# Moving the sums of x for u's seven products from VectorE to GpSimd, and writing variance plus epsilon as a scalar_tensor_tensor

## The chip, the cores and the metric

The kernel runs on one core of a Trainium2 chip. The metric is the device time of one execution in microseconds (us); lower is better. The engines are named as the profile names them: PE is the matrix engine (TensorE), PEld its loading of weights, DVE is VectorE, ACT is ScalarE, POOL is GpSimd, and SP issues DMAs.

## The reference

A linear attention without softmax, with a normalisation per head, feeds a gated layer with a spatial product. All tensors are float32.

```python
kv = np.einsum('bhsd,bhse->bhde', k, v)          # 8 batches, 8 heads, 576 rows, 64 columns
out = np.einsum('bhsd,bhde->bhse', q, kv)
rms = np.sqrt(np.mean(out * out, axis=-1, keepdims=True) + 1e-06)
x = out / rms * g_norm                            # then [8, 576, 512]
h = np.maximum(x @ w_in, 0.0)                     # 512 -> 1024
u, v = h[..., :512], h[..., 512:]
v_n = (v - mean(v)) / np.sqrt(var(v) + 1e-06)
v_s = np.einsum('ts,bsd->btd', w_spatial, v_n) + b_spatial[None, :, None]
out = (u * v_s) @ w_out
```

## The kernel before

**Precision.** Most products are made three times from a high and a low half of each operand (names ending in H and L). `split` makes the halves: ACT casts the high half (L327), DVE subtracts it for the low half (L328).

**Stages.** From batch b = 2 on, each batch runs through three stages on PE. `first(b)` makes v (`hv`, L324, PSUM tile `psh`) and u (`u_steps`, L546, tiles `psua`, `psub`, `psuc`). `second(b)` makes the spatial product (`sp_steps`, L546, L552 and L554, tiles `psa`, `psb`, `psc`) and `gate`s it with u into G (L565, L567, then a split). `last(b)` multiplies G by the output weights WO (`out_unit`, L291, shown as `pso<-WO,G`; each unit has four steps of K, three products each) and stores. The attention of later batches (L136, L211, and transposes L239 and L249 into `pstr` and `pstt`) is threaded between these steps.

**The sums of x.** u's products and the spatial products are made with seven block products instead of eight, by adding and subtracting blocks first. For u these are blocks of x: `x_sums_` runs once for each of the batches 2 to 7, with two rounds (k = 0, 1) of eight instructions on 128x288 blocks: four sums XH+XL (L440) into tiles p1, u2, u3 and g, then four differences (L442 to L445). Then `split` puts the results into T (L327 and L328, tile T, with a part of it in tile UX). T lies in the buffer of G, and UX in the buffer of WO, so the splits, and the DMA UX<-spare_u (L871, issued on POOL), wait until the out stage of the batch before has read G and WO for the last time. PE first reads T in `psub<-T` (L546), after `hv` and the first step of u.

**The normalisations.** `rsqrt_a` computes 1/sqrt(variance + epsilon): ACT takes the square root (L173), DVE adds epsilon (L174) and takes the reciprocal (L175), and `rsqrt_b` refines it (L180 to L182). It runs on 128x8 tiles for the heads and on 128x1 tiles for the layer norm.

**Order.** The first two batches follow a table (PLAN); the rest is written as loops. A scheduler that keeps a timeline of its own then sets the order of the instructions on each engine. `tc.issue_after(last_gate[0])` puts the sums behind a gate's last DVE instruction in that scheduler. Each engine runs its instructions strictly in the order given, so changed costs on one engine can change the order on all of them.

Of the kernel before, what the change touches and what calls it, by code (L numbers as in the profile page):

```python
# [8 lines left out]
F32 = mybir.dt.float32  # L9
# [4 lines left out]
ALU = mybir.AluOpType  # L14
# [5 lines left out]
P = 128  # L20
# [10 lines left out]
EPS = 1e-6  # L31
# [13 lines left out]
def f32(ap):  # L45
    return ap.bitcast(F32)
# [3 lines left out]
def body(ctx: ExitStack, tc, qT, kvm, kvt, g2, w_in, wsT, bsp, w_out, out):  # L50
    nc = tc.nc
# [48 lines left out]
    ident = persistent([P, P], F32, "ident")  # L100
    gcol = persistent([P, 16], F32, "gcol")[:, 0:1]
    edge = ctx.enter_context(tc.tile_pool(name="edge", bufs=1, side="right"))
    epsc = edge.tile([P, 8], F32, name="epsc", tag="epsc")[:, 0:1]

# [59 lines left out]
    def rsqrt(ss, n, rows, mul, tag):  # L166

        return rsqrt_b(*rsqrt_a(ss, n, rows, mul, tag))

    def rsqrt_a(ss, n, rows, mul, tag):  # L170
        a, s0, q, r = (small.tile([P, n], F32, name=f"{x}{tag}", tag=f"{x}{tag}")[0:rows]
                       for x in "asqr")
        nc.scalar.activation(s0, ss, AF.Sqrt, bias=epsc[0:rows], scale=mul)  # L173
        nc.vector.tensor_scalar(a, ss, mul, EPS, op0=ALU.mult, op1=ALU.add)  # L174
        nc.vector.reciprocal(q, a)  # L175
        return s0, q, r

# [10 lines left out]
    def norm_a(ps, rows=P, accumulate=False):  # L188
        x = work.tile([P, 512], F32, name="x", tag="x")[0:rows]
        ss = small.tile([P, 8], F32, name="ss", tag="ss")[0:rows]  # L190
        if accumulate:
            for h in range(8):
                cols = slice(h * D, (h + 1) * D)
                nc.scalar.activation(x[:, cols], ps[0:rows, cols], AF.Square,  # L194
                                     accum_out=ss[:, h:h + 1])
        else:
            nc.scalar.activation(x, ps[0:rows], AF.Square)
            nc.vector.tensor_reduce(ss, heads(x), axis=AX.X, op=ALU.add)
        return ps, x, rows, rsqrt_a(ss, 8, rows, 1.0 / D, "h")
# [126 lines left out]
    def split(hi, lo, x):  # L326
        nc.scalar.copy(hi, x)  # L327
        nc.vector.tensor_tensor(lo, x, f32(hi), op=ALU.subtract)  # L328
# [100 lines left out]
    def x_sums():  # L429

        with tc.issue_after(last_gate[0]):
            x_sums_()

    def x_sums_():
        for k in range(2):
            q = []
            for of, j, name in ((0, 0, "p1"), (2, 1, "u2"), (0, 1, "u3"), (2, 0, "g")):
                q.append(work.tile([P, HS], F32, name=name, tag=name))
                x = [f32(x[:, of + k, j * HS:(j + 1) * HS]) for x in (XH, XL)]
                nc.vector.tensor_tensor(q[-1], *x, op=ALU.add)  # L440
            q11, q22, q12, q21 = q
            nc.vector.tensor_tensor(q11, q12, q11, op=ALU.subtract)  # L442
            nc.vector.tensor_tensor(q12, q22, q12, op=ALU.subtract)
            nc.vector.tensor_tensor(q22, q22, q11, op=ALU.subtract)
            nc.vector.tensor_tensor(q21, q21, q22, op=ALU.subtract)  # L445
            for n, x in (1, q22), (0, q11), (2, q12), (3, q21):
                split(TH[n][:, k], TL[:, n, k], x)

# [340 lines left out]
        issue()  # L789

    nc.vector.memset(KVB[:, 1], 0.0)
    nc.vector.memset(epsc, EPS)
    nc.scalar.activation(small.tile([P, 1], F32, name="warm", tag="av"), epsc, AF.Sqrt)
    nc.gpsimd.memset(KVB[:, 0], 0.0)
    for kt in KT:
# [227 lines left out]
```

## Time and profile before

| | |
|---|---|
| median of 3 runs | 512.02 us (511.95 to 512.6) |
| the profiled execution's own time | 511.49 us |
| its span (first to last instruction) | 509.7 us |
| granted PE clock, mean | 0.998 |
| busy PE, DVE, ACT, POOL | 499.0, 411.5, 291.9, 21.4 us |

Sums and waits below come from this one profiled execution. Rows of the timeline give start, duration, engine, line and operation, with the idle time before it and what ended that in brackets. Rows of groups give the count, the busy time, the mean of one in ns, and the idle time before. Pipelined instructions overlap, so the distance between two starts is less than the duration of one.

### The profile page before, as it was taken

How to read it: one execution, taken by the hardware profiler on the slowest of the kernel's cores; microseconds unless marked ns; L12 is line 12 of the kernel's file. 1: busy time of each engine (PE TensorE's matmuls, PEld its weight loads, DVE VectorE, ACT ScalarE, POOL GpSimd, SP SyncE). 2: the span in 40 equal slices, each digit the busy share in tenths (PEclk: the TensorE clock that was granted, in tenths of full speed). 3: DMA queues.
4: the chain of work that ended last, by engine and by line, in shares of the span. 5: the costliest groups of instructions: out<-in, count | busy, mean ns of one | idle time of the engine just before them, and what ended most of it. 6: DMA issues, size and time to landing. Idle time of an engine off the chain costs nothing.

```text
span 509.7 us, 9917 instructions
## 1 busy us (share of the span) xinstructions
PE 499.0 (98%) x3436; PEld 439.0 (86%) x3436; DVE 411.5 (81%) x1265; ACT 291.9 (57%) x1021; POOL 21.4 (4%) x47
## 2 busy tenths in 40 slices
PE   7999999999999999999999999999999999999996
PEld 6658788898988899989998899988998889988995
DVE  3898599688998699968897779968898579987860
ACT  2555456896734696457732688447642578527422
POOL 5000000000000001000000001000000001000000
PEclk9999999999999999999999999999999999999999
DMA  8995300735346516345265514424354511314223
GB/s 254 330 339 191 100 24 1 236 91 176 116 152 209 186 42 212 118 117 174 76 218 196 187 42 154 152 91 164 123 178 146 167 39 44 145 42 165 70 98 104
DMA packets 28071, 72.24 MB, mean 142 GB/s; under 512 B 3506, under 2 KB 8626, under 8 KB 26484
## 3 DMA queue, kind: packets, MB, share of 16 engines
q1 hardware_dynamic: 24564, 49.58, 29.9%
q0 software_dynamic: 3456, 22.02, 12.6%
q8 instruction: 27, 0.44, 0.4%
q14 instruction: 24, 0.20, 0.1%
HBM read 58.48 MB, written 13.11 MB: 140 GB/s over the span
## 4 chain that ended last, share of the span: by engine, by line
PE 78%; ACT 8%; DVE 7%; DMA 4%; POOL 1%; issue 1%; SPq 0%; ACTq 0%; POOLq 0%; DVEq 0%
PE pso L291 15%; PE psh L324 12%; PE psb L546 6%; PE psub L546 5%; PE pso L211 5%; PE psc L546 4%; PE pskv L136 3%; PE psa L546 3%; PE psua L546 3%; PE psuc L546 3%; PE psu L402 3%; PE psa L411 3%; PE psh L378 3%; PE pstr L239 2%; ACT x L194 2%; DMA out<-o 1%
## 5 line engine op out<-in xcount | busy, mean ns | idle before, releaser
L291 PE MATMUL pso<-WO,G 128*128 128x512 f32 x384 | 97.3, 396 | 0.0
L291 PEld LDWEIGHTS pso<-WO,G 128*128 128x128 f32 x384 | 70.3, 188 | 14.1
L327 ACT CAST G<-g 128x288 fp32r<-128x288 f32 (+1 forms) x56 | 22.8, 408 | 61.2 <-DVE g L567 60.8
L194 ACT ACTIVATE x<-pso 128x64 f32<-128x64 f32 x208 | 44.3, 252 | 5.5 <-PE pso L211 5.3
L324 PE MATMUL psh<-WVL,XH 128*128 128x512 f32 x112 | 43.7, 390 | 0.0
L324 PE MATMUL psh<-WVH,XH 128*128 128x512 f32 x112 | 43.6, 393 | 0.0
L194 ACT ACTIVATION_READ_ACCUMULATOR x<-pso 128x1 f32 x208 | 43.5, 238 | 0.0
L324 PE MATMUL psh<-WVH,XL 128*128 128x512 f32 x112 | 43.4, 392 | 0.0
L328 DVE TENSOR_TENSOR VL<-v,VH 128x512 fp32r<-128x512 f32 (+1 forms) x56 | 34.2, 619 | 7.8 <-ACT VH L327 7.6
L648 ACT COPY o<-pso 128x512 f32<-128x512 f32 x35 | 20.3, 593 | 26.0 <-PE pso L291 23.5
L327 ACT CAST VH<-v 128x512 fp32r<-128x512 f32 (+1 forms) x56 | 31.1, 574 | 4.2 <-DVE v L356 3.8
L303 DVE BATCH_NORM_STATS2 s<-v 128x6 f32<-128x512 f32 x32 | 21.8, 690 | 7.3 <-ACT v L297 7.1
L546 PE MATMUL psb<-WSH,VH 128*128 128x288 f32 x84 | 25.4, 304 | 0.2
L311 ACT ACTIVATE v<-v,mv,rv 128x512 f32<-128x512 f32 x28 | 23.2, 837 | 3.2 <-DVE mv L310 3.2
L324 PEld LDWEIGHTS psh<-WVH,XH 128*128 128x128 f32 x112 | 21.0, 188 | 4.6 <-ACT o L648 0.2
L297 ACT ACTIVATE v<-psh 128x512 f32<-128x512 f32 x32 | 18.7, 595 | 10.9 <-PE psh L324 7.6
L324 PEld LDWEIGHTS psh<-WVL,XH 128*128 128x128 f32 x112 | 21.0, 188 | 4.6
L324 PEld LDWEIGHTS psh<-WVH,XL 128*128 128x128 f32 x112 | 21.0, 188 | 4.4
L546 PE MATMUL psb<-WSL,VH 128*128 128x288 f32 x84 | 24.6, 295 | 0.0
L546 PE MATMUL psb<-WSH,VL 128*128 128x288 f32 x84 | 24.3, 297 | 0.1
L328 DVE TENSOR_TENSOR G<-g,G 128x288 fp32r<-128x288 f32 (+1 forms) x56 | 23.4, 418 | 1.1 <-ACT G L327 0.4
L136 PEld LDWEIGHTS pskv<-KV 128*64 128x64 f32 x512 | 18.1, 140 | 6.7 <-issue 2.9
(243 smaller groups left out, 1426.2 us busy)
## 6 DMA issues: line engine op xcount, KB each, us to landing
KV<-kvm SPq DMA_DIRECT2D x31, 512.0 KB, 5.1
WO<-spare_o POOLq DMA_DIRECT2D x12, 1024.0 KB, 6.6
UX<-spare_u POOLq DMA_DIRECT2D x12, 768.0 KB, 6.0
out<-o SPq DMA_DIRECT2D x32, 256.0 KB, 2.2
qt<-qT SPq DMA_DIRECT2D x16, 288.0 KB, 4.3
stage<-w_in SPq DMA_DIRECT2D x8, 512.0 KB, 6.4
qt<-qT SPq DMA_DIRECT2D x16, 256.0 KB, 2.9
KT<-kvt SPq DMA_DIRECT2D x32, 64.0 KB, 4.7
```

What stands on the lines that cost most here:

```text
L136: return nc.tensor.matmul(ps[h:h + D, at:at + D], of[:, 0, h:h + D], of[:, 1, h:h + D], start=c == 0, stop=c == NC)
L194: nc.scalar.activation(x[:, cols], ps[0:rows, cols], AF.Square, accum_out=ss[:, h:h + 1])
L211: nc.tensor.matmul(ps[:, c * P:(c + 1) * P], qt[:, c * P:(c + 1) * P], st[p], start=True, stop=True)
L291: nc.tensor.matmul(ps, lt, rh, start=i == 0, stop=i == n - 1)
L297: nc.scalar.activation(v, ps, AF.Relu)
L303: nc.vector.bn_stats(s6, v)
L311: nc.scalar.activation(v, v, AF.Identity, bias=m, scale=r)
L324: nc.tensor.matmul(ps, lt, rh, start=k == 0 and i == 0, stop=k == NP - 1 and i == 2)
L327: nc.scalar.copy(hi, x)
L328: nc.vector.tensor_tensor(lo, x, f32(hi), op=ALU.subtract)
L546: nc.tensor.matmul(ps, lt, rh, start=start and i == 0, stop=stop and i == len(pairs) - 1, skip_group_check=True)
L648: nc.scalar.copy(o, ps)
```

## The change

The eight sums and differences of each round of `x_sums_` are issued on GpSimd instead of VectorE. In `rsqrt_a`, the tensor_scalar that multiplies by `mul` and adds the constant epsilon becomes a scalar_tensor_tensor that multiplies by `mul` and adds a tile `epsn` of 8 columns, which a memset fills with epsilon. All lines below the first edit move down by one: L440 of before is L441 after it.

```diff
-    epsc = edge.tile([P, 8], F32, name="epsc", tag="epsc")[:, 0:1]
+    epsn = edge.tile([P, 8], F32, name="epsc", tag="epsc")
+    epsc = epsn[:, 0:1]
...
-        nc.vector.tensor_scalar(a, ss, mul, EPS, op0=ALU.mult, op1=ALU.add)
+        nc.vector.scalar_tensor_tensor(a, ss, mul, epsn[0:rows, 0:n], op0=ALU.mult, op1=ALU.add)
...
-                nc.vector.tensor_tensor(q[-1], *x, op=ALU.add)
+                nc.gpsimd.tensor_tensor(q[-1], *x, op=ALU.add)
             q11, q22, q12, q21 = q
-            nc.vector.tensor_tensor(q11, q12, q11, op=ALU.subtract)
-            nc.vector.tensor_tensor(q12, q22, q12, op=ALU.subtract)
-            nc.vector.tensor_tensor(q22, q22, q11, op=ALU.subtract)
-            nc.vector.tensor_tensor(q21, q21, q22, op=ALU.subtract)
+            nc.gpsimd.tensor_tensor(q11, q12, q11, op=ALU.subtract)
+            nc.gpsimd.tensor_tensor(q12, q22, q12, op=ALU.subtract)
+            nc.gpsimd.tensor_tensor(q22, q22, q11, op=ALU.subtract)
+            nc.gpsimd.tensor_tensor(q21, q21, q22, op=ALU.subtract)
...
-    nc.vector.memset(epsc, EPS)
+    nc.vector.memset(epsn, EPS)
```

The scheduler moves instructions on every engine. On POOL, between the out stage of batch 1 and that of batch 3, before:

```order
L871 DMA UX<-spare_u 128x1536 x2
L263 CAST XL<-XL 128x4x64
L877 DMA WO<-spare_o 128x2048 x2
L871 DMA UX<-spare_u 128x1536 x2
L877 DMA WO<-spare_o 128x2048 x2
```

and now, for batch 3 (the end of the 16 sums; names as u_2707 carry a buffer's number):

```order
L445 TENSOR_TENSOR u_2687<-u_2687,p_2685 128x288
L441 TENSOR_TENSOR u_2709<-XH,XL 128x288
L441 TENSOR_TENSOR p_2705<-XH,XL 128x288
L443 TENSOR_TENSOR p_2705<-u_2709,p_2705 128x288
L441 TENSOR_TENSOR g<-XH,XL 128x288
L441 TENSOR_TENSOR u_2707<-XH,XL 128x288
L446 TENSOR_TENSOR g<-g,u_2687 128x288
L444 TENSOR_TENSOR u_2709<-u_2707,u_2709 128x288
L441 TENSOR_TENSOR g<-XH,XL 128x288
L445 TENSOR_TENSOR u_2707<-u_2707,p_2705 128x288
L446 TENSOR_TENSOR g<-g,u_2707 128x288
L872 DMA UX<-spare_u 128x1536 x2
```

All 16 sums of a batch now stand ahead of its DMA UX<-spare_u on POOL.

On PE, in the out stage that comes just before batch 3 reads T (pso_2649 and pso_2665 are the units of the row blocks 2 and 3), before:

```order
L291 MATMUL pso_2665<-WO,G 128x512 x3
L324 MATMUL psh<-WVH,XH 128x512
L324 MATMUL psh<-WVL,XH 128x512
L324 MATMUL psh<-WVH,XL 128x512
L324 MATMUL psh<-WVH,XH 128x512
L324 MATMUL psh<-WVL,XH 128x512
L291 MATMUL pso_2649<-WO,G 128x512 x2
L291 MATMUL pso_2665<-WO,G 128x512 x2
L324 MATMUL psh<-WVH,XL 128x512
L324 MATMUL psh<-WVH,XH 128x512
L324 MATMUL psh<-WVL,XH 128x512
L291 MATMUL pso_2649<-WO,G 128x512 x7
```

and now:

```order
L292 MATMUL pso_2649<-WO,G 128x512 x3
L212 MATMUL pso<-KVB,qt 128x128 x3
L292 MATMUL pso_2665<-WO,G 128x512 x3
L292 MATMUL pso_2649<-WO,G 128x512 x9
L292 MATMUL pso_2665<-WO,G 128x512 x9
L325 MATMUL psh<-WVH,XH 128x512
L325 MATMUL psh<-WVL,XH 128x512
```

The eight products of `psh` that stood inside the out units now follow them, so the last reading of G comes earlier in the order.

On PE, at the start of the spatial stage of batch 1 (131 us in the profile), before:

```order
L546 MATMUL psb<-WSL,VH 128x288
L546 MATMUL psb<-WSH,VL 128x288
L239 MATMUL pstr<-ident,x 128x128 x4
L546 MATMUL psa<-WSH,VH 128x288
L546 MATMUL psa<-WSL,VH 128x288
L546 MATMUL psa<-WSH,VL 128x288
```

and now:

```order
L547 MATMUL psb<-WSL,VH 128x288
L547 MATMUL psb<-WSH,VL 128x288
L547 MATMUL psc<-WSH,VH 128x288
L547 MATMUL psc<-WSL,VH 128x288
L547 MATMUL psc<-WSH,VL 128x288
L547 MATMUL psc<-WSH,VH 128x288
```

The transposes `pstr` moved behind some 60 further products, and the products of `psc` follow `psb` at once.

## The prediction

> **What bounds the kernel now.** I read the busy shares first, then the sums by stretch, then PE's own timeline around the places where the change acts.
>
> ```profile
> PE 499.0 (98%) x3436; PEld 439.0 (86%) x3436; DVE 411.5 (81%) x1265; ACT 291.9 (57%) x1021; POOL 21.4 (4%) x47
> core 0: us, PE busy (x) PEld busy (x) DVE busy (x) ACT busy (x) POOL busy (x), PEclk, DMA share, GB/s
> ...
> 150.00:505.80 355.80, 355.03 (x2467) 322.14 (x2465) 288.92 (x910) 202.38 (x732) 14.11 (x27) 1.00 0.40 131
> 505.80:509.70 3.90, 0.00 (x0) 0.00 (x0) 0.42 (x1) 0.29 (x1) 0.00 (x0) 0.77 0.42 147
> ...
> 129.00:146.00 17.00, 15.99 (x134) 14.72 (x135) 16.70 (x48) 9.43 (x25) 0.00 (x0) 1.00 0.37 125
> ...
> 212.10:219.80 7.70, 7.70 (x48) 6.86 (x47) 7.70 (x27) 4.48 (x30) 0.00 (x0) 1.00 0.39 134
> ```
>
> From 150 us on PE is idle for 355.80 - 355.03 = 0.77 us by its busy time, and the last 3.9 us are the final store. So the six batches that hold the moved sums are bound by PE, and relief of DVE cannot give much there. DVE is full in two kinds of places: for 16.70 of 17.00 us in the spatial stage of batch 1, and for all 7.70 us in which the sums of batch 3 run. Only the first of these makes PE wait.
>
> **Term 1, the sums leave DVE.**
>
> ```profile
> L440 DVE TENSOR_TENSOR u<-XH,XL 128x288 f32<-128x288 f32 x24 | 10.3, 452 | 0.0
> L444 DVE TENSOR_TENSOR u<-u,p 128x288 f32<-128x288 f32 x12 | 5.2, 441 | 0.0
> 212.19 0.45 DVE L440 TENSOR_TENSOR p<-XH,XL 128x288 f32<-128x288 f32 x1
> 212.55 0.82 DVE L440 TENSOR_TENSOR u<-XH,XL 128x288 f32<-128x288 f32 x2
> 219.31 0.46 DVE L445 TENSOR_TENSOR g<-g,u 128x288 f32<-128x288 f32 x1
> ```
>
> One takes 0.45 us and the next starts 0.36 us later (212.19 to 212.55). Sixteen per batch are 16 x 0.36 = 5.8 us, six batches 35 us of DVE time. Almost none of it lies on the path: the sums of batch 3 end at 219.77, and the next step cannot use them yet.
>
> ```profile
> 226.19 1.05 POOL L871 DMA_DIRECT2D UX<-spare_u  x2 [30.98 <-PE pso L291]
> 226.41 0.44 ACT L327 CAST T<-u 128x288 fp32r<-128x288 f32 x1
> 229.08 1.11 ACT L297 ACTIVATE v<-psh 128x512 f32<-128x512 f32 x2
> 228.36 0.45 DVE L328 TENSOR_TENSOR T<-u,T 128x288 fp32r<-128x288 f32 x1
> 222.46 3.43 PE L291 MATMUL pso<-WO,G 128*128 128x512 f32 x14
> 234.83 0.29 PE L546 MATMUL psua<-XH,WUH 128*128 128x288 f32 x1
> 236.41 0.42 PE L546 MATMUL psub<-T,WUH 128*128 128x288 f32 x2
> ```
>
> The casts into T start at 226.41, when the out stage's last products (222.46 + 3.43 = 225.89) have released G. So the finished sums lie unused for 226.41 - 219.77 = 6.6 us. PE reads T only at 236.41, 8 us after the split it needs most (round 1's, which starts at 228.36).
>
> **Term 2, the sums on POOL.** No two-input operation of POOL is in this trace. The nearest rows:
>
> ```profile
> L263 POOL CAST XL<-XL 128x256 fp32r<-128x256 f32 x3 | 1.3, 428 | 79.6 <-PE psuc L546 55.2 <-issue 24.4
> L798 POOL MEMSET KVO<- 128x256 f32 x2 | 0.6, 320 | 0.1
> L794 POOL MEMSET KVB<- 128x128 f32 x1 | 0.2, 205 | 0.3 <-POOLq L1012 0.3
> ```
>
> The memsets give (320 - 205)/128 = 0.9 ns per column and about 90 ns fixed. One input adds 108 ns on 256 columns, 0.42 ns per column. A second input that only adds as much gives 90 + 288 x 1.74 = 590 ns, the lower end. Two inputs at twice the whole cast give 2 x 428 x 288/256 = 963 ns, the upper end. I take 0.75 us with its handover, nearer the lower end because the cast shows that an input adds less than it would alone. Sixteen take 12 us. From the same start the sums of batch 3 end at 212.2 + 12 = 224.2, still before 226.4; at the upper end at 227.6, 1.2 us behind it. In the new order eight `psh` products (0.23 us each, 3.43 us for 14) leave the out stage, so G comes free about 1.9 us sooner, at 224.0, and the casts then wait for POOL instead of PE, by little.
>
> What is late next: ACT holds the first relu of `psh` behind the casts of T, and `psua` needs a PSUM bank that this relu frees. Before, the relu starts at 229.08 and `psua` at 234.83, so the casts may slip by about 5 us. The split for `psub` may slip by 236.41 - 228.81 = 7.6 us. The DMA UX<-spare_u now stands behind the sums on POOL; PE needs UX after T. So the cover is gone only when the sums end later than about 233.7, that is at (233.7 - 212.2)/16 = 1.34 us each. Below that I cost this term at nothing.
>
> The Trainium skill (GPSIMD Engine Reference, section 3.1) speaks against such a move: it has elementwise work with two inputs 1.96 times as slow on GpSimd as on VectorE. By that, as an estimate, one sum takes 1.96 x 0.45 = 0.88 us and sixteen take 14 us, which lies inside my ends and changes no term.
>
> **Term 3, DVE and POOL in each other's way.**
>
> ```profile
> 193.12 0.69 DVE L328 TENSOR_TENSOR VL<-v,VH 128x512 fp32r<-128x512 f32 x1
> 193.72 0.36 DVE L181 SCALAR_TENSOR_TENSOR qh<-sh,rh 128x8 f32<-128x8 f32 x1
> 193.58 0.48 POOL L263 CAST XL<-XL 128x256 fp32r<-128x256 f32 x1 [24.44 <-issue]
> L181 DVE SCALAR_TENSOR_TENSOR qh<-sh,rh x40: 151/160/361, 13.0 to 439.4; 128x8 f32<-128x8 f32 x40
> L174 DVE TENSOR_SCALAR ah<-ss x40: 156/166/174, 12.2 to 437.8; 128x8 f32<-128x8 f32 x40
> ```
>
> One L181 of 40 took 361 ns where the median is 160: the one that met the POOL cast. It ended at 194.08, when the cast ended (194.06). The cast itself, begun under a DVE subtraction, took 0.48 us where its mean is 0.43. So an instruction with two SBUF inputs on DVE and a reading one on POOL do not run together.
>
> A rule of the Trainium skill (SBUF — State Buffer, section "Who interferes with whom") says just that: a DVE instruction with two SBUF inputs contends with a GpSimd instruction that reads SBUF, and one waits for the whole of the other. The row agrees (0.20 us lost).
>
> Within the sums' stretch of batch 3 DVE has seven more instructions with two SBUF inputs (one L567, two L328, L180 to L182, and L174 in its new form). Each waits at most one sum, 0.75 us: at most 5.3 us, below the 5.8 us that left. So DVE is not worse off over the stretch; what counts is the last gate.
>
> ```profile
> 154.00 0.29 PE L554 MATMUL psc<-WTL,TB 128*128 128x288 f32 x1
> 154.33 0.46 DVE L565 TENSOR_TENSOR g<-psc,u 128x288 f32<-128x288 f32 x1
> 155.44 0.45 DVE L567 SCALAR_TENSOR_TENSOR g<-U,g 128x288 f32<-128x288 f32 x1
> 156.57 1.63 PE L291 MATMUL pso<-WO,G 128*128 128x512 f32 x6
> 156.91 0.39 DVE L328 TENSOR_TENSOR G<-g,G 128x224 fp32r<-128x224 f32 x1
> ```
>
> This is batch 1, the tightest of the six in the new order. Before, sums stood between L565 and L567; without them L567 starts at 154.8 and the low half of G is there at 157.3 - 0.65 = 156.65. In the new order the products that read it follow the six of 156.57 after six more, at about 159.3. L567 and L328 can lose at most 2 x 0.75 = 1.5 us of the 2.7 us between. I take 0.3 us for places I did not see, from 0 to 1.5 us.
>
> **Term 4, epsilon by scalar_tensor_tensor.** The old form took 166 ns and L181, a scalar_tensor_tensor of the same size, 160: 40 x 6 ns, nothing. The 128x1 form is as short. The memset of 8 columns instead of one stands at the start, where PE waits for its first loads anyway. What this edit does is change the scheduler's order, in the spatial stage of batch 1 above all.
>
> **Term 5, PE's waits under a new order.**
>
> ```profile
> 131.28 0.29 PE L546 MATMUL psb<-WSL,VH 128*128 128x288 f32 x1
> 131.66 0.40 PE L546 MATMUL psb<-WSH,VL 128*128 128x288 f32 x1
> 132.26 0.66 PE L239 MATMUL pstr<-ident,x 128*128 128x128 f32 x4 [0.20 <-DVE x L203]
> 143.80 0.29 PE L554 MATMUL psb<-WTL,TB 128*128 128x288 f32 x1
> 144.68 0.63 PE L249 MATMUL pstt<-ident,x 128*128 128x128 f32 x4 [0.59 <-DVE x L203]
> 195.95 0.29 PE L546 MATMUL psa<-WSH,VL 128*128 128x288 f32 x1
> 196.68 0.63 PE L239 MATMUL pstr<-ident,x 128*128 128x128 f32 x4 [0.44 <-DVE qh L175]
> ```
>
> Products of 288 columns start every 0.13 us when nothing is late. So PE loses 0.25 us before 131.66, 0.47 before 132.26, 0.75 before 144.68 and 0.60 before 196.68: 2.1 us, all on DVE. The change moves the transposes of 132.26 far behind, and lets DVE subtract VL first. But DVE is full there and keeps its work, so the wait can come back where `pstr` and `pstt` now stand. Ends: nothing, and 1.47 us for the three in batch 1. I take 0.9, nearer the upper end because the order gives DVE what PE asks for next. For 196.68 and smaller waits in later spatial stages I take 0.5 of some 1.5.
>
> **The sum:** -0.9 - 0.5 + 0.3 = -1.1 us. The profiled execution took 511.49 (span 509.7 and 1.8 around it), which gives 510.4; it lay 0.5 us under the median of 512.02, against which the change is timed, so I forecast 512.0 - 1.1 = 510.9.
>
> **The rivals.**
> - *The waits only move; the rest is hidden.* DVE keeps all its work in the spatial stages, and its relief falls where PE never waited: 512.0. For it speaks the 6.6 us in which finished sums lie unused; against it, that the transposes left the place of their wait.
> - *POOL ends the stage (slower).* If a sum with its waits takes over 1.34 us, the odd batches 3, 5 and 7 wait; at 1.6 us by 16 x 1.6 - 21.5 = 4.1 us each, 12 us in all: 523. Against it: the upper end of the rows is 0.96, and seven meetings with DVE subtractions of 0.45 us add 0.2 each, 1.16.
> - *The lock costs PE (slower).* If L567, L328 or the normalisations wait for POOL in series and lose 3.2 us instead of 2.7 us, PE stands for 0.5 us in each of six batches: 512.0 - 1.4 + 3 = 513.6. It decides from 2.7 us of loss on a last gate. The row of 193.72 speaks for the mechanism, the count of two instructions against the size.
> - *All of PE's waits on DVE go*: 2.1 us and some small ones, 509.5.
>
> **How the numbers follow.** Of three runs before, two lie within 0.1 us and one 0.6 us higher; 0.2% (1.0 us) is about what a measurement here can tell. Forecast 0.48 (0.38 of it beyond 1.0 us, 0.10 within), waits move 0.27 (same), lock 0.12 (0.09 slower, 0.03 same), POOL late 0.06 (slower), all waits gone 0.07 (faster). That is 0.45 faster, 0.40 same, 0.15 slower. The forecast alone spans 510.0 to 511.5; the range takes in "all gone" at its low end and the lock at its high end: 509.0 to 513.4.
>
> **What would show it.** Sums on POOL of 0.6 to 0.95 us each; the sums of batch 3 done before 229; no idle time of PE before `psub<-T`; DVE instructions of L567 and L328 with single durations near 1 us under the sums; at the `psc` products that follow `psb` in batch 1 no wait, and `pstt` starting within 0.5 us of the product ahead. A PE wait on POOL, or one on G in the out stages, would make it wrong.

## The result: 0.7% slower

The changed kernel takes 515.5 us (median of 4 runs, 515.02 to 516.5) against 512.16 for the kernel before beside it: a ratio of 1.0071, interval 1.0053 to 1.0089. That is 3.3 us slower, where 1.1 us faster was forecast. The profiled execution took 515.02 us (span 513.1), 3.5 us more than the one of before.

The page and the sums by stretch of the changed kernel (all its lines from L104 on are one higher than before):

```profile
PE 499.6 (97%) x3436; PEld 437.5 (85%) x3436; DVE 408.8 (80%) x1169; ACT 293.7 (57%) x1021; POOL 104.7 (20%) x143
```

```profile
core 0: us, PE busy (x) PEld busy (x) DVE busy (x) ACT busy (x) POOL busy (x), PEclk, DMA share, GB/s
150.00:505.80 355.80, 354.61 (x2462) 321.13 (x2462) 286.97 (x820) 203.92 (x731) 94.04 (x120) 1.00 0.39 130
146.00:150.00 4.00, 3.05 (x47) 2.15 (x46) 4.00 (x12) 1.73 (x5) 2.49 (x3) 1.00 0.58 182
```

The first surprise stands in the first row. The 96 sums had cost DVE some 35 us (96 x 0.36), and they are gone (1265 instructions became 1169), yet DVE's busy time fell by 2.7 us only, from 411.5 to 408.8. Something gave the time back. The groups of DVE, by shape, say what (busy us, then mean ns of one):

```profile
L568 DVE SCALAR_TENSOR_TENSOR g<-U,g 128x288 f32<-128x288 f32 x42 | 27.0, 650 | 0.3
L329 DVE TENSOR_TENSOR G<-g,G 128x224 fp32r<-128x224 f32 x28 | 16.9, 605 | 2.8 <-ACT G L328 2.5
L329 DVE TENSOR_TENSOR G<-g,G 128x288 fp32r<-128x288 f32 x28 | 16.3, 582 | 0.0
L566 DVE TENSOR_TENSOR g<-psc,u 128x288 f32<-128x288 f32 x28 | 12.6, 449 | 2.2 <-PE psc L555 1.9
L329 DVE TENSOR_TENSOR GT<-g,GT 128x64 fp32r<-128x64 f32 x28 | 12.4, 442 | 0.0
L568 DVE SCALAR_TENSOR_TENSOR g<-U,psa 128x288 f32<-128x288 f32 x14 | 6.2, 440 | 0.8 <-PE psa L555 0.7
```

The same view of the kernel before:

```profile
L567 DVE SCALAR_TENSOR_TENSOR g<-U,g 128x288 f32<-128x288 f32 x42 | 18.3, 450 | 0.1
L328 DVE TENSOR_TENSOR G<-g,G 128x288 fp32r<-128x288 f32 x28 | 12.6, 451 | 0.0
L328 DVE TENSOR_TENSOR G<-g,G 128x224 fp32r<-128x224 f32 x28 | 10.8, 384 | 1.1 <-ACT G L327 0.4
L328 DVE TENSOR_TENSOR GT<-g,GT 128x64 fp32r<-128x64 f32 x28 | 6.1, 217 | 0.0
```

The gate's product and its splits took 18.3 + 12.6 + 10.8 + 6.1 = 47.8 us and now take 72.6: 24.8 of the 35 us came back here, in four groups whose inputs all lie in SBUF. Another 4.9 us came back in the 128x8 instructions of the normalisations (L174, L180 and L181 of before, 19.5 us; the same lines now, 24.4 us). The groups with one input from PSUM (`psc`, `psa`) kept their 0.44 to 0.45 us. The same line L568 stretches with g and does not with `psa`, so it is not the operation but where its second input lies.

Where it reaches PE is seen in the timelines of DVE, POOL and PE at the end of batch 6's spatial stage:

```profile
446.05 0.58 DVE L568 SCALAR_TENSOR_TENSOR g<-U,g 128x288 f32<-128x288 f32 x1
446.56 1.07 DVE L329 TENSOR_TENSOR G<-g,G 128x288 fp32r<-128x288 f32 x1
447.65 0.45 DVE L568 SCALAR_TENSOR_TENSOR g<-U,psa 128x288 f32<-128x288 f32 x1
448.03 0.74 DVE L234 SCALAR_TENSOR_TENSOR XL<-pstr,gcol,XH 128x512 fp32r<-128x512 f32 x1
```

```profile
445.27 1.04 POOL L443 TENSOR_TENSOR p<-u,p 128x288 f32<-128x288 f32 x1
446.27 1.03 POOL L441 TENSOR_TENSOR u<-XH,XL 128x288 f32<-128x288 f32 x1
447.38 0.89 POOL L444 TENSOR_TENSOR u<-u,u 128x288 f32<-128x288 f32 x1
```

```profile
446.18 0.29 PE L555 MATMUL psc<-WTL,TB 128*128 128x288 f32 x1
446.31 0.86 PE L292 MATMUL pso<-WO,G 128*128 128x512 f32 x3
448.16 2.31 PE L292 MATMUL pso<-WO,G 128*128 128x512 f32 x8 [1.00 <-DVE g L568]
```

The split at 446.56 should take 0.45 us. It takes 1.07 and ends at 447.63, 0.33 us after the sum of 446.27. The gate behind it is late, and PE stands 1.00 us. In the kernel before, PE runs from the same `psc` into the products of `pso` without a stop:

```profile
444.16 0.29 PE L554 MATMUL psc<-WTL,TB 128*128 128x288 f32 x1
444.30 2.92 PE L291 MATMUL pso<-WO,G 128*128 128x512 f32 x12
```

### The profile page after: what moved, and what is told of

Same layout as the page of the kernel before. It is cut to its first block, busy times and chain, and to the rows that moved or that the text cites. A ratio compares the mean times of both kernels' runs of the same rounds, so it can differ in the third digit from the quotient of the medians.

```text
span 513.1 us, 9930 instructions
## 1 busy us (share of the span) xinstructions
PE 499.6 (97%) x3436; PEld 437.5 (85%) x3436; DVE 408.8 (80%) x1169; ACT 293.7 (57%) x1021; POOL 104.7 (20%) x143
## 4 chain that ended last, share of the span: by engine, by line
PE 87%; ACT 4%; DMA 3%; DVE 3%; issue 1%; SPq 0%; ACTq 0%
PE pso L292 19%; PE psh L325 13%; PE psub L547 6%; PE psb L547 5%; PE pso L212 5%; PE psc L547 4%; PE pskv L137 4%; PE psua L547 4%; PE psuc L547 4%; PE psa L547 4%; PE psu L403 3%; PE psa L412 3%; PE psh L379 3%; PE pstr L240 2%; PE psu L292 2%; DMA KV<-kvm 2%
## 5 line engine op out<-in xcount | busy, mean ns | idle before, releaser
L328 ACT CAST G<-g 128x288 fp32r<-128x288 f32 (+1 forms) x56 | 22.7, 406 | 70.3 <-DVE g L568 70.2
L441 POOL TENSOR_TENSOR p<-XH,XL 128x288 f32<-128x288 f32 x12 | 11.2, 936 | 153.3 <-DVE g L566 139.6
L649 ACT COPY o<-pso 128x512 f32<-128x512 f32 x35 | 20.1, 592 | 27.6 <-PE pso L292 18.3
L329 DVE TENSOR_TENSOR G<-g,G 128x288 fp32r<-128x288 f32 (+1 forms) x56 | 33.2, 594 | 2.8 <-ACT G L328 2.5
L328 ACT CAST VH<-v 128x512 fp32r<-128x512 f32 (+1 forms) x56 | 31.3, 569 | 3.4 <-DVE v L357 2.4
L441 POOL TENSOR_TENSOR u<-XH,XL 128x288 f32<-128x288 f32 x24 | 21.5, 904 | 39.6 <-DVE rh L183 23.1
L568 DVE SCALAR_TENSOR_TENSOR g<-U,g 128x288 f32<-128x288 f32 x42 | 27.0, 650 | 0.3
```

The costliest lines, as they stand in the source:

```text
L441: nc.gpsimd.tensor_tensor(q[-1], *x, op=ALU.add)
L568: nc.vector.scalar_tensor_tensor(g, U[:, d, cols], 0.0, ps, op0=ALU.max, op1=ALU.mult)
```

## The experiments

All edits are against the kernel before, unless said otherwise. "Order" below means the row-by-row order of the instructions on an engine. Lines are numbered as before. Edits are shown in part, with `...` for what is left out. Three theories: A, the sums on GpSimd hold up DVE's instructions with SBUF inputs (the lock); B, the order that the epsilon edit sets off costs the time; C, the order that the sums' move sets off costs it.

**The epsilon edit alone.**

```diff
...
-        nc.vector.tensor_scalar(a, ss, mul, EPS, op0=ALU.mult, op1=ALU.add)
+        nc.vector.scalar_tensor_tensor(a, ss, mul, epsn[0:rows, 0:n], op0=ALU.mult, op1=ALU.add)
...
```

> The kernel before with the epsilon edit alone (scalar_tensor_tensor for variance plus epsilon, 8 columns of epsilon); the sums stay on VectorE. Theory A (lock): what the change lost comes from GpSimd's sums holding up VectorE instructions with two SBUF inputs, so this edit is worth nothing: 512.2, within 0.5 us of before, and the gates keep 0.45 us each. Rival B (order): the edit changes PE's order in the spatial stage of batch 1 and ACT's around 87 us, and of the 3.3 us the changed kernel loses, the 1.0 to 1.2 us that it has lost by 147 us come from here: 513.2.

Measured: 514.19 us, ratio 1.0044 (1.0030 to 1.0058), so 2.0 us slower, more than B had it. The instruction is no longer than the old one (median 162 ns), but PE's timeline has three waits that are shorter or absent before:

```profile
88.05 1.20 PE L324 MATMUL psh<-WVH,XH 128*128 128x512 f32 x4 [0.46 <-ACT WVH L707]
...
105.16 0.40 PE L291 MATMUL psu<-XH,WUH 128*128 128x288 f32 x1 [0.82 <-ACT v L297]
...
147.97 1.40 PE L291 MATMUL pso<-WO,G 128*128 128x512 f32 x5 [0.94 <-DVE g L565]
```

**The edit at 75 of 76 places.** In the program's twelfth place the old form stays; PE's order is then that of before.

> The kernel before with the epsilon edit at 75 of its 76 places; one, the twelfth in the program (a 128x8 of batch 1's normalisation, at 60 us), keeps the tensor_scalar. With it PE's order is again that of the kernel before, row for row. If the edit costs by the order it sets off (what the edit alone showed: waits of 0.62 us at 87 us, 0.98 at 104 and 1.01 at 147 that are not in before), the time is 512.2, within 0.5 of before, and those waits are gone. If the new instruction itself costs, it is 514.2 as with all 76.

Measured: 511.64 us, ratio 0.9991 (0.9983 to 1.0000). One instruction of 0.16 us, left in its old form, takes away the whole loss. So the new instruction costs nothing, and the order costs 2.0 us.

**The sums alone**, run twice:

```diff
-                nc.vector.tensor_tensor(q[-1], *x, op=ALU.add)
+                nc.gpsimd.tensor_tensor(q[-1], *x, op=ALU.add)
...
-            nc.vector.tensor_tensor(q11, q12, q11, op=ALU.subtract)
+            nc.gpsimd.tensor_tensor(q11, q12, q11, op=ALU.subtract)
...
```

> The kernel before with the sums on GpSimd alone; epsilon in its old form. Theory A (lock): the gates of the batches with sums stretch as in the changed kernel (mean of the gate's scalar_tensor_tensor near 0.65 us instead of 0.45), and the time is 514 to 515.5, that is 1.5 us or more above before. Rival B (order by the epsilon edit): a third or more of the loss is gone, below 514.5. Rival C (the sums' leaving reorders PE, the lock costs nothing): also 515, told apart by the next two.

> The sums-alone kernel once more, beside the kernel with memsets. Lock theory: 515 by its median, and again a wait of PE of about 1.2 us at 446 us on a gate, with gates of a mean of 0.65 us, in this second profile too; if that wait was chance, it is not there.

Measured: 515.3 us, ratio 1.0063 (1.0042 to 1.0084), and 515.8, 1.0070 (1.0052 to 1.0087). The old epsilon saves nothing here, so B as a whole explanation falls. In both profiles PE waits at the same place as in the changed kernel. From the second:

```profile
449.38 0.97 PE L291 MATMUL pso<-WO,G 128*128 128x512 f32 x3 [0.99 <-DVE g L567]
```

Under this order PE also stands 0.69 us on G in batch 1 (156.6 us; 0.74 in the first profile), which it does not in the changed kernel.

**The changed kernel without its sums, and with memsets in their place.** In the second, each sum is two memsets:

```diff
-                nc.gpsimd.tensor_tensor(q[-1], *x, op=ALU.add)
+                nc.gpsimd.memset(q[-1], 0.5)
+                nc.gpsimd.memset(q[-1], 0.5)
...
```

> The changed kernel with the sixteen sums of each batch left out (T and UX are split from XH as it stands, so that u is not what the reference computes); PE's order is the changed kernel's, instruction for instruction, and GpSimd has no sums. Theory A (lock): the gates go back to 0.45 us, PE's waits at 147, 217, 335 and 447 us go, and the time falls by 2 us or more from 515.5, to 511.0 to 513.3. Rival C (the new order of PE costs the time): the waits stay without any sum, 515 or more.

> The changed kernel with each sum replaced by two memsets of the same tile on GpSimd, which write and read nothing (so u is not what the reference computes); the order on PE, VectorE and ScalarE is the changed kernel's. GpSimd is busy for 11 to 13 us per batch at the same places. Theory A in its form 'only a reading GpSimd holds VectorE up': gates at 0.45 us and the time as without sums, 511.0 to 513.3. If a writing GpSimd holds it up as well: gates with single durations of 0.6 to 0.8 us and a time between that and 515.5. Rival C: 515.

Measured: 513.2 us (1.0017, 1.0001 to 1.0034) without sums, 513.09 (1.0021, 1.0008 to 1.0034) with memsets. Both are 2.3 to 2.4 us under the changed kernel by the medians (2.6 to 2.8 by the ratios). PE's order is the same in all three, and with memsets so are DVE's and ACT's. With memsets POOL still works beside the gates (32 x 0.34 = 10.8 us per batch), and DVE's gates are whole again:

```profile
L567 DVE SCALAR_TENSOR_TENSOR g<-U,g x42: 441/451/460, 143.0 to 497.9; 128x288 f32<-128x288 f32 x42
```

```profile
L439 POOL MEMSET u<- 128x288 f32 x24 | 8.1, 339 | 188.0 <-DVE g L565 188.0
```

In the changed kernel the 31 gates that overlap a sum take 0.72 us on the mean and the other 11 take 0.45; here 36 of the 42 overlap memsets, and they take 0.45. PE goes through 446 us without a stop, while the wait at 147 us stays (148.27, 0.94 us on g). Start by start, PE in the changed kernel falls behind the one with memsets by 0.3 us at 217 us, 0.3 at 335 and 1.5 from 446 to 450. So the reading sums cost 2.3 us (A). What is left, 1.0 us, is the new order together with what DVE's relief gives back under it. The epsilon edit's order alone cost 2.0, and the two were not told apart here.

**The same control with the old epsilon.** First no sums at all:

> The kernel with the sums on GpSimd and the old epsilon, its sixteen sums left out (u is not what the reference computes); the order on PE is that of the sums-alone kernel, row for row. It shows what the order and the relief of VectorE are worth with no lock and without the epsilon edit. Lock theory: 2.0 to 2.3 us under the sums-alone kernel, so 512.6 to 513.3 by its median of 515.3, or about 512 by its profiled run, of whose loss 1.1 us was one late load at 33 us; the wait of 1.16 us at 446 us is gone. If the order costs and not the lock: 515.

Measured: 514.42 us (1.0038, 1.0017 to 1.0059), its runs from 510.78 to 515.86: not what A expected. The profiled run (512.75 us) has no wait at 446 us, but another one, on ScalarE in the out stage of batch 1:

```profile
171.33 0.59 ACT L648 COPY o<-pso 128x512 f32<-128x512 f32 x1 [3.63 <-DMA out<-o]
```

A buffer of the output was still being stored, and PE then stood 1.13 us at 183 us for a copy of ScalarE. With memsets instead of sums, so that POOL issues its loads as late as with sums:

> The kernel with the sums on GpSimd and the old epsilon, each sum replaced by two memsets of the same tile, which read nothing (u is not what the reference computes). PE, VectorE and ScalarE have the order of the sums-alone kernel, row for row, and GpSimd is busy at the same places, so that it issues the load of UX about as late; without any sums that load came early, a store of the out stage landed late, and ScalarE stood 3.6 us for it. Lock theory: as with the new epsilon, where memsets took 2.4 us off, so 2.0 us or more below the sums run beside it; the wait at 446 us is gone. If it ends within 0.7 us of the sums, the lock is not what the sums alone cost, but their order.

Measured: 513.36 us (1.0028, 1.0016 to 1.0040), 2.4 us under the sums run beside it, and no wait at 446 us or on G in batch 1. By the medians the sums cost about as much under this order as under the other. The late loads did not remove the other wait, though: here too ScalarE stands for a store (2.09 us, before 171.95) and PE 1.14 us for ScalarE at 183.77. So the store does not set the two kernels apart. The intervals of their ratios overlap, and why the one without sums has the higher median stays open.

**The sums held until the last gate is through**, so that nothing of a gate meets them:

```diff
+        flag = nc.gpsimd.tensor_copy(small.tile([P, 1], F32, name="flag", tag="flag"), f32(last_gl[0][:, 0:1])).ins
-        with tc.issue_after(last_gate[0]):
+        with tc.issue_after(last_gate[0]), tc.issue_after(flag):
...
```

> The changed kernel with the sums held on GpSimd until the last gate of the batch is through: a copy of one column of GT, which the last gate writes, stands ahead of them on GpSimd. Nothing is left out. Sixteen sums of 0.85 us then run beside the out stage, end at about 230 in batch 3, and the casts into T slip by some 3 us, which the 8 us before PE reads T cover. Lock theory: the gates are back at 0.45 us and the time is that without sums, 513.2, within 0.8. If the order alone costs, or the casts' slip reaches PE: 515 or more. The scheduler also moves other rows, which may cost or give some tenths.

> The same hold, with the old epsilon: the sums on GpSimd after the last gate, and nothing else changed against the kernel before. If both causes are what the runs so far say (the lock under the gates 2.0 to 2.3 us, the epsilon edit's order 1 to 2 us), this has neither and comes to 511.2 to 512.5, at or a little under the kernel before; otherwise 513.5 or more.

Measured: a ratio of 1.0228 (1.0186 to 1.0269), 11.7 us above before, with single runs from 519.46 to 530.91; and, with the old epsilon, 529.15 us (1.0335, 1.0319 to 1.0351). The lock theory missed by more than 10 us. The other outcomes that were named, 515 or more and 513.5 or more, were laid to the order or to late casts, not to a longer hold. The sums now run in one row, and DVE, here with the old epsilon, shows this:

```profile
402.83 8.54 DVE L174 TENSOR_SCALAR ah<-ss 128x8 f32<-128x8 f32 x1
...
412.39 0.69 DVE L203 TENSOR_TENSOR x<-pst,rh 128x512 f32<-128x512 f32 x1
```

```profile
399.06 0.80 POOL L440 TENSOR_TENSOR p<-XH,XL 128x288 f32<-128x288 f32 x1
...
408.25 1.60 POOL L444 TENSOR_TENSOR u<-u,p 128x288 f32<-128x288 f32 x2
409.77 1.57 POOL L445 TENSOR_TENSOR g<-g,u 128x288 f32<-128x288 f32 x2
```

A 128x8 instruction of 0.17 us took 8.54 and ended when the last sum did (411.34). Eleven sums passed in that time, not one. PE stood 3.84 us for it:

```profile
413.23 0.63 PE L249 MATMUL pstt<-ident,x 128*128 128x128 f32 x4 [3.84 <-DVE x L203]
```

Ten shorter waits of PE after 140 us, 0.4 to 1.4 us each and mostly on ScalarE, add 8.4 us. They were not traced back.

**A fixed order of the held sums, round by round, without and with a memset after each** (old epsilon; the sums' lines are one higher in these two):

```diff
...
+                chain(nc.gpsimd.tensor_tensor(q[-1], *x, op=ALU.add)); chain(nc.gpsimd.memset(small.tile([P, 64], F32, name='gap', tag='gap'), 0.0))
...
```

> The held sums of the last kernel (old epsilon, sums after the last gate), with their order on GpSimd fixed: eight of round 0, then eight of round 1, back to back. The kernel with held sums was 17 us slower, and in its trace single 128x8 instructions of VectorE took 4.2, 5.2 and 8.5 us, each ending with a row of back-to-back sums. Theory D (train): a VectorE instruction that loses SBUF to GpSimd does not get it back after one sum; it waits until GpSimd pauses. With the same train: again single durations of 3 us and more on VectorE, and 518 to 530. Rival E (a sum each): no VectorE instruction loses more than 0.85 us, and the time of the held kernel came from its order; round by round the casts into T start sooner, so 513 to 516.

> The same order with a memset of 128x64 (it reads nothing) after each sum on GpSimd, some 0.15 us each, so that GpSimd works longer by 2.4 us per batch. Theory D (train): each memset lets VectorE in, no VectorE instruction is stretched by more than one sum (below 1.1 us for a 128x8), and although GpSimd has more to do the time falls by 4 us or more against the kernel without the memsets. Rival E: the same time or slower than without the memsets, since the sums end later.

Measured: 519.07 us (1.0150, 1.0123 to 1.0177) without the memsets, 522.07 (1.0202, 1.0172 to 1.0233) with them. Neither theory holds as written. D's time for the first came true, but not its durations: no DVE instruction lost much more than one sum (the longest took 1.54 us), though the row again has sixteen sums. With memsets the time rose by 3.0 us, as E had it, yet one instruction still took 4.77:

```profile
349.45 4.77 DVE L328 TENSOR_TENSOR T<-p,T 128x288 fp32r<-128x288 f32 x1
354.14 1.06 DVE L328 TENSOR_TENSOR T<-u,T 128x288 fp32r<-128x288 f32 x1
```

```profile
349.70 0.82 POOL L441 TENSOR_TENSOR p<-XH,XL 128x288 f32<-128x288 f32 x1
...
353.01 0.14 POOL L441 MEMSET gap<- 128x64 f32 x1
353.11 0.79 POOL L443 TENSOR_TENSOR p<-u,p 128x288 f32<-128x288 f32 x1
...
353.98 0.91 POOL L444 TENSOR_TENSOR u<-u,u 128x288 f32<-128x288 f32 x1
```

Five sums passed, with memsets between them, before DVE got in, about when the sum of 353.98 starts, which overwrites what the one ahead reads. In the kernel without memsets a sum that hangs on the one ahead starts 0.88 us after it, and independent ones start 0.77 apart:

```profile
222.54 0.80 POOL L443 TENSOR_TENSOR p<-u,p 128x288 f32<-128x288 f32 x1
223.42 0.81 POOL L444 TENSOR_TENSOR u<-u,u 128x288 f32<-128x288 f32 x1
...
225.95 0.81 POOL L441 TENSOR_TENSOR p<-XH,XL 128x288 f32<-128x288 f32 x1
226.72 1.57 POOL L441 TENSOR_TENSOR u<-XH,XL 128x288 f32<-128x288 f32 x2
```

These rows suggest that POOL lets DVE in where it has to wait for something, and that a memset in between does not do it. Others speak against it. In the held kernel with the new epsilon, a 128x8 instruction came through at the loss of one sum, while the sums followed each other without a pause:

```profile
222.70 0.72 DVE L181 SCALAR_TENSOR_TENSOR qh<-sh,rh 128x8 f32<-128x8 f32 x1
```

```profile
221.84 1.55 POOL L440 TENSOR_TENSOR u<-XH,XL 128x288 f32<-128x288 f32 x2
223.36 0.80 POOL L440 TENSOR_TENSOR g<-XH,XL 128x288 f32<-128x288 f32 x1
```

And in batch 3 of the kernel with memsets, splits into T lost one independent sum each (230.73, 1.06 us). What makes a hold last one sum or many stays open.

## Why the prediction was wrong

**The account.** Before 512.2; the new order, with no sums on GpSimd or memsets in their place, 513.1 to 513.2 (+1.0); the lock, 515.5 (+2.3). The forecast was -1.4 for the order and +0.3 for the lock. So two terms of the sum failed: the order's by its sign, since it counted only the waits that go, and the lock's by its size, since the sums were taken to start behind the gates.

**What bounds the kernel: right.** From 150 us on PE idles 355.80 - 354.61 = 1.2 us (0.8 before). Idle time shows only a part of the 2.3 us: from 446 to 450 us the starts of PE's products slip by 1.5 us against the kernel with memsets, and 1.00 of it is seen as idle. Relief of DVE did not make up for the new order: with all sums left out, the kernel is still 1.0 us slower than before.

**Term 1 (the sums leave DVE): right in what left, but most of it came back.** "Finished sums lie unused" held.

**Term 2 (the sums on POOL): the price about right, the start wrong.** POOL's seven groups of sums add up to 85.0 us, of which the first and the last by busy time are:

```profile
L441 POOL TENSOR_TENSOR u<-XH,XL 128x288 f32<-128x288 f32 x24 | 21.5, 904 | 39.6 <-DVE rh L183 23.1 <-DVE XL L234 12.5 <-DVE g L566 4.0
L445 POOL TENSOR_TENSOR u<-u,p 128x288 f32<-128x288 f32 x12 | 9.8, 813 | 0.3
```

One takes 85.0 / 96 = 0.89 us on the mean, inside the ends, where 0.75 was taken. The Trainium skill's figure (GPSIMD Engine Reference, section 3.1) gave 0.88 as an estimate, and this trace agrees on the mean; a sum that met no VectorE instruction took 0.80 us (399.06 above). The casts into T start at 226.26, PE does not wait there, and so POOL does not end the stage, as argued. But the step "from the same start" failed. The first sum of batch 3 starts at 205.44 instead of 212.19. That the last one ends at 223.9, where 224.2 was forecast, is luck: with the waits between them the sixteen take 18.4 us, not 12. `issue_after` queues instructions of DVE behind a gate; on POOL nothing held the sums back, and they began as soon as x and a buffer were there, under the last gates.

**Term 3 (the lock): the mechanism right, the size wrong, and with it the forecast.** It follows from the start. "Seven more instructions" and "L567 and L328 can lose at most 2 x 0.75" counted the stretch in which DVE used to make the sums, behind the gates. In the changed kernel 31 of the 42 gates with two SBUF inputs overlap a sum. "I take 0.3" measured 2.3. What held is that a gate loses no more than about one sum (the longest of the 42 took 1.08 us). Batch 1 as "the tightest of the six" was wrong in this kernel: there PE, by its timeline, runs from the last `psc` (156.18) into nine products of the out stage without a stop, in batch 6 only three (446.31) stand ahead of the one that waits. Of the rival *the lock costs PE* the cause came true, but not its place: not 0.5 us in each of six batches, but 1.5 us in batch 6 and 0.3 in batches 2 and 4. Its 513.6 also lay just outside the stated range, which was to take it in. The Trainium skill (SBUF — State Buffer, "Who interferes with whom") has the lock last for one whole instruction; the rows at 446 us agree, the row of 8.54 us does not.

**Term 4 (epsilon): right as an instruction, and its real effect named but not priced.** 75 of 76 new instructions cost nothing; the order that the edit sets off costs 2.0 us alone.

**Term 5 (PE's waits under a new order): the wrong sign.** What it said would shrink did: `pstt` starts 0.35 us after the product ahead (145.03, 145.38) instead of 0.88, and the 0.6 us at 196 us is gone. But only the waits that would go were counted. New ones came where the forecast did not look: 0.46 us on WVH at 88 us and 0.95 on v at 105, where ACT does other work first, and 0.95 on g at 148 us, with DVE full (4.00 of 4.00 us). The last of them in the changed kernel:

```profile
148.27 1.82 PE L292 MATMUL pso<-WO,G 128*128 128x512 f32 x6 [0.95 <-DVE g L566]
```

The wait at 148 us is also in the epsilon edit alone, which has no sum on POOL, so it is the order's and not the lock's. "One on G in the out stages would make it wrong": it did.

## What to carry to other kernels

Work given to GpSimd is priced by what DVE does meanwhile, and it starts where its own queue lets it: ask what holds it back on the new engine before counting what it meets. A scheduler that orders by its own timeline can answer an edit that costs nothing with microseconds; run the new order by itself, with the moved work left out or replaced by memsets, before crediting or blaming the work. When counting the waits that an order removes, look for those that it makes, over the whole program.

## What the runs showed of the hardware

- A GpSimd instruction that reads SBUF holds up a VectorE instruction with two SBUF inputs, memsets of the same tiles do not (0.65 against 0.45 us on the mean of 42 gates). VectorE instructions with one input from PSUM are untouched (0.45 us). A tensor_scalar with one SBUF input was held too (8.54 us).
- The hold can last over many GpSimd instructions: 8.54 us of one 0.17 us instruction under eleven sums in one row. In the same series of runs others lost a single sum under such rows (0.72 us at 222.70), and what decides was not found.
- After PE stood 3.84 us, its clock was granted at half for some 3 us more, by the sums by stretch of the held kernel (old epsilon); the 1 us wait at 448 us of the changed kernel left it at 1.00.

```profile
413.00:414.00 1.00, 0.78 (x5) 0.73 (x6) 0.08 (x1) 0.11 (x1) 0.00 (x0) 0.90 0.00 0
414.00:415.00 1.00, 1.00 (x4) 0.78 (x3) 0.48 (x1) 0.36 (x1) 0.00 (x0) 0.50 0.00 0
...
416.00:417.00 1.00, 1.00 (x3) 0.72 (x3) 0.47 (x2) 1.00 (x4) 1.00 (x2) 0.50 0.00 0
417.00:418.00 1.00, 1.00 (x5) 0.85 (x4) 1.00 (x3) 1.00 (x4) 0.02 (x1) 0.90 1.15 100
```
